# Retention and two MoE layers on one core: the retention's 64x64 matmuls in four quarters of the array, two fixed banks, and two weight tiles fetched earlier

## The chip, the core and the metric

The kernel runs on one core of one Trainium2 chip. The metric is the device time of one execution in microseconds (us). The core's engines are TensorE (PE, with its weight loads shown apart as PEld), VectorE (DVE), ScalarE (ACT), GpSimd (POOL) and SyncE (SP); here SP issues all transfers.

## The reference

What is computed, cut to the core (float32 throughout):

```
scores = q @ k.T / sqrt(64)                      # batch 8, heads 8, sequence 576, head size 64
gamma  = 1 - 2 ** (-5 - head)
ret    = (scores * where(i >= j, gamma ** (i - j), 0)) @ v       # retention, causal with decay
x   = ret, heads side by side                                    # (4608, 512)
h   = max(x @ w1, x @ w2, x @ w3)                                # 512 -> 768
x   = h @ w_out                                                  # 768 -> 512
h   = x @ w_in                                                   # 512 -> 2048
out = (h * clip(h + 3, 0, 6) / 6) @ w_out2                       # 2048 -> 512
```

The weights arrive as float64 words, and the kernel turns them into pairs of float32 parts on the chip.

## The kernel before

**Retention.** A unit is one batch and one pair of heads (e = 0, 1): 8 batches x 4 pairs = 32 units. The sequence is cut into nine chunks of C = 64 positions. For each chunk and head there are three kinds of 64x64 products: *scores* (keys times queries, L217), *outer* products (keys times values, the chunk's contribution to the running state, L225), and *values* (L260: masked scores and old state, stacked to 128 rows, times values and queries). Between them DVE multiplies the scores by a mask (`masked`, L238), adds up the states one chunk after the other (`states`, L251 and L253), and scales the result (`decayed`, L264).

The two heads of a unit lie in the two halves of a tile `raw` (128 partitions). A 64x64 matmul uses one quarter of the 128x128 array: the half of the rows is that of the partitions its operands lie in, the half of the columns is that of the PSUM partitions it writes. Writing (row, column) for a quarter's first row and column, scores of e = 0 and 1 lie in (64, 0) and (0, 64), and outer products of e = 1 and 0 lie in (64, 0) and (0, 64) as well. `keys(n)` issues, chunk by chunk for four chunks, two scores and two outer products, all into bank `at`n, four chunks of scores in its left half and four of outer products in its right half. A matmul of `values` takes all 128 rows and one half of the columns.

The first four units (class `Summed`) run by themselves at the start. Each of the other 28 is done in three steps, `first` (keys(0)), `second` (keys(1), values of chunks 0 to 3, scores of chunk 8) and `third` (values of chunks 4 to 8); the third step of a unit is issued right behind the first step of the next. Between steps stand blocks of twelve 128x512 matmuls of the first MoE layer (`up`, `down`, L393 to L395). In stage t (a tile of 512 tokens) the MoE blocks of tile t are interleaved with the retention of batch t+1: stage 0 with batch 1, stage 1 with batch 2, stages 2 to 6 with batches 3 to 7. What each engine does stands in program order; nothing is reordered by a planner.

**What a step waits for.** PSUM tiles are banks of 512 columns. Waits are set per bank: DVE may read a bank only behind the last matmul issued into it, and the reverse. In before, keys(1) goes into `at1`, and values and scores of chunk 8 into a new tile in `at0`. A unit's `raw` tile (two buffers) is loaded by SP behind the third step of the unit before the last, and ACT scales its keys (`decay`, L188) before the outer products may start.

**Weights.** A class `Weights` fetches float64 tiles (`ws`, three buffers, L93) and turns them into float32 pairs in a pipeline of DVE, ACT and POOL. `wa` does the first layer's 24 tiles during stage 0. `wb_part` does the second layer's 32 tiles; its steps are called by `background()` at every fourth block of stages 1 to 6. Its first step comes at the start of stage 1 and fetches its own first two tiles; on SP they stand behind the four stores `x2d<-y` of tile 0, and DVE's L110 waits for them.

Of the kernel before, what the change touches and what calls it, by code (L numbers as in the profile page):

```python
# [7 lines left out]
F32 = mybir.dt.float32  # L8
# [22 lines left out]
VS1, Z0, KT, KN = 0, S, 2 * S, 3 * S  # L31
# [5 lines left out]
def retention_moe_moe2(ctx: ExitStack, tc, hi, lo, w_a, w_b, mask, qdec, kdec, grow, out):  # L37
    nc = tc.nc
# [33 lines left out]
    def acc_tiles():  # L72
        return [ps_acc.tile([P, 512], F32, tag=f"o{m}", name=f"o{m}") for m in range(4)]
# [3 lines left out]
    mask_sb = at.tile([P, HP, C], F32, name="mask_sb")  # L77
# [60 lines left out]
    def pair():  # L138
        return moe.tile([P, 2, 512], F32R, tag="hy", bufs=8, name="y")
# [7 lines left out]
    wb_part = Weights(w_b, order_b, lambda i: pair())  # L147
# [4 lines left out]
    halves = (slice(0, D), slice(D, P))  # L152
# [32 lines left out]
    def decay(i):  # L185
        if i < len(units):
            k = raws[i][:, KN:HI]
            nc.scalar.mul(k, k, kdec_sb[:, units[i][1], 0:1])  # L188

    xs, xe, ys = {}, {}, {}  # L190

    class Unit:

        def __init__(self, i, banks=None):
            self.i = i
            self.b, self.hp = units[i]
            self.banks = banks

        def begin(self):
            self.ps = self.banks or [ps_at.tile([P, 512], F32, tag=f"at{n}", name=f"at{n}") for n in range(2)]

        def again(self, n):
            if not self.banks:
                self.ps[n] = ps_at.tile([P, 512], F32, tag=f"at{n}", name=f"at{n}")

        def part(self, e, c, first, second):

# [3 lines left out]
        def scores(self, c, ps, c0):  # L213
            t = raws[self.i]
            for e in range(2):
                own, other = halves[e], halves[1 - e]
                nc.tensor.matmul(ps[own, c0:c0 + C], lhsT=t[other, KT + c * C:KT + (c + 1) * C],  # L217
                                 rhs=self.part(e, c, Z0, Z1)[other, :], start=True, stop=True)

        def outer(self, c, ps, c0):  # L220
# [5 lines left out]
                                 rhs=self.part(e, c, VS0, VS1)[own, :], start=True, stop=True)  # L226

        def keys(self, n):
            for c in range(4):
                self.scores(4 * n + c, self.ps[n], c * C)  # L230
                self.outer(4 * n + c, self.ps[n], (4 + c) * C)

        def masked(self, c, n, ps, p0):
            t = raws[self.i]
            for e in range(2):
                own = halves[e]
                c0 = (Z0, Z1)[e] + c * C
                nc.vector.tensor_tensor(  # L238
                    out=t[own, c0:c0 + n * C].rearrange("p (c s) -> p c s", s=C),
                    in0=ps[own, p0:p0 + n * C].rearrange("p (c s) -> p c s", s=C),  # L240
                    in1=mask_sb[own, self.hp, None, :].to_broadcast([D, n, C]), op=ALU.mult)

        def states(self, n):
            for c in range(4 * n, 4 * n + 4):
                for e in range(2):
                    other = halves[1 - e]
                    new, old = (self.part(e, c + d, VS0, VS1)[other, :] for d in (1, 0))
                    c0 = (4 + c - 4 * n) * C
                    add = self.ps[n][other, c0:c0 + C]
                    if c == 0:  # L250
                        nc.vector.tensor_copy(new, add)  # L251
                    else:
                        nc.vector.scalar_tensor_tensor(  # L253
                            out=new, in0=old, scalar=gamma[2 * self.hp + e] ** C, in1=add, op0=ALU.mult, op1=ALU.add)
# [13 lines left out]


        def first_mm(self):  # L270
            self.begin()
            self.keys(0)

        def first_rest(self):
# [2 lines left out]

        def second_mm(self):
            self.keys(1)
            self.again(0)  # L280
            self.values(range(4), self.ps[0])
            self.scores(NC - 1, self.ps[0], 4 * C)

        def second_rest(self):
            self.masked(4, 4, self.ps[1], 0)
            self.states(1)
            self.masked(NC - 1, 1, self.ps[0], 4 * C)
            self.y = at.tile([P, S], F32, tag="yr", bufs=2, name="yr")
            self.decayed(0, 4, self.ps[0])

        def third_mm(self):
            self.again(1)
            self.values(range(4, NC), self.ps[1])

        def third_rest(self):
            self.decayed(4, NC - 4, self.ps[1])
            self.finish()

        def finish(self):
# [8 lines left out]
    class Summed(Unit):  # L308

        def __init__(self, i, banks):
            super().__init__(i, banks)

        def prepare(self):
            for c in range(NC - 1):
                k = raws[self.i][:, KN + c * C:KN + (c + 1) * C]
                nc.scalar.mul(k, k, kdec_sb[:, self.hp, c:c + 1])

        def keys_mm(self):  # L320
            self.begin()
            t = raws[self.i]
            for c in range(NC - 1):
                self.scores(c, self.ps[0], c * C)
            for c in range(NC - 1):
                for e in (1, 0):
                    own, other = halves[e], halves[1 - e]
                    n = NC - 1 - c
                    nc.tensor.matmul(
                        self.ps[1][other, c * C:].rearrange("p (n d) -> p n d", d=D),  # L330
                        lhsT=t[own, KN + c * C:KN + (c + 1) * C],
                        rhs=self.part(e, c, VS0, VS1)[own, None, :].to_broadcast([C, n, D]),
                        start=(c == 0), stop=(c == NC - 2))
# [10 lines left out]
                    in1=grow_sb[other, self.hp, :, None].to_broadcast([D, NC - 1, D]), op=ALU.mult)  # L344

        def values_mm(self):
            self.scores(NC - 1, self.ps[1], 0)
            self.values(range(NC - 1), self.ps[0])

        def values_rest(self):  # L350
            self.masked(NC - 1, 1, self.ps[1], 0)
            self.y = at.tile([P, S], F32, tag="yr", bufs=2, name="yr")
            self.decayed(0, NC - 1, self.ps[0])

        def last_mm(self):
            self.values([NC - 1], self.ps[1], C)

        def last_rest(self):
            self.decayed(NC - 1, 1, self.ps[1], C)
            self.finish()  # L360

    def steps(b):

        us = [Unit(b * HP + hp) for hp in range(HP)]
        res = []
        for hp in range(HP + 1):
            u, last = (us[hp] if hp < HP else None), (us[hp - 1] if hp else None)

            def begin(u=u, last=last):
                if u:  # L370
                    u.first_mm()
                if last:
                    last.third_mm()
                if u:
                    u.first_rest()
                if last:
                    last.third_rest()
                load_raw(b * HP + hp_of(u, last) + 1)

            res.append(begin)  # L380
            if u:
                res.append(lambda u=u: (u.second_mm(), u.second_rest(), decay(u.i + 1) if u.hp < HP - 1 else None))
        return res

    def hp_of(u, last):
        return u.hp if u else HP
# [59 lines left out]
    with tc.manual_schedule():  # L446
# [11 lines left out]
        nc.scalar.mul(rebias, rebias, 2.0 ** 23)  # L458
        xs[0] = x_tile()
        spare = acc_tiles()  # L460
        pairs = [[ps_at.tile([P, 512], F32, tag=f"at{n}", name=f"at{n}") for n in range(2)], spare[:2], spare[2:],
                 [ps_mm.tile([P, 512], F32, tag="mm", name="mm") for n in range(2)]]
        us = [Summed(i, pairs[i]) for i in range(HP)]
        wa.step()
# [23 lines left out]
        def prepare(t):  # L488

            if t >= B:  # L490
                return []
            xs[t] = x_tile()
            decay(t * HP)
            return steps(t)


        side = prepare(1)
        ahead = [lambda f=f, j=j: up(1, f, j) for f in range(3) for j in range(3)]
        for n, blk in enumerate(blocks(0) + [lambda: down(0, F1 - 1)]):
            while wa.steps < min(n + 3, NA + 2):  # L500
                wa.step()
            blk()
            if wa.steps < NA + 2:
                wa.step()
            if side:
                side.pop(0)()
            elif n >= 11 and ahead and n * 9 // 13 > (n - 1) * 9 // 13:
                ahead.pop(0)()
        while ahead:
            ahead.pop(0)()  # L510
# [17 lines left out]
        for t in range(1, TT):  # L528
            side = prepare(t + 1)
# [95 lines left out]
        for t in range(TT):  # L625
            for f in range(F2):
                if f == 4:
                    load_x2(t + 1)
                ps = hidden(t, f)
# [68 lines left out]
```

## Time and profile before

| | |
|---|---|
| median of 3 runs | 1586.28 us (1585.41 to 1587.09) |
| the profiled execution's own time | 1587.3 us |
| its span, first to last instruction | 1585.2 us |
| mean granted TensorE clock | 0.989 |
| busy: PE, PEld, DVE, ACT, POOL | 97%, 79%, 49%, 21%, 10% of the span |

Busy shares are means over stages that differ: at the start transfers and DVE set the pace, later TensorE. A busy PE is not an engine at its peak, since matmuls are pipelined and several can be in flight. Each float32 matmul leaves two records on PE (and two weight loads on PEld), so "x4" in a row of L217 is two matmuls; the MoE's matmuls leave one.

### The profile page before, as it was taken

How to read it: one execution, taken by the hardware profiler on the slowest of the kernel's cores; microseconds unless marked ns; L12 is line 12 of the kernel's file. 1: busy time of each engine (PE TensorE's matmuls, PEld its weight loads, DVE VectorE, ACT ScalarE, POOL GpSimd, SP SyncE). 2: the span in 40 equal slices, each digit the busy share in tenths (PEclk: the TensorE clock that was granted, in tenths of full speed). 3: DMA queues.
4: the chain of work that ended last, by engine and by line, in shares of the span. 5: the costliest groups of instructions: out<-in, count | busy, mean ns of one | idle time of the engine just before them, and what ended most of it. 6: DMA issues, size and time to landing. Idle time of an engine off the chain costs nothing.

```text
span 1585.2 us, 22461 instructions
## 1 busy us (share of the span) xinstructions
PE 1541.1 (97%) x9376; PEld 1257.9 (79%) x9376; DVE 775.4 (49%) x1641; ACT 330.2 (21%) x601; POOL 155.0 (10%) x180
## 2 busy tenths in 40 slices
PE   7789899999999999999999999999999999999998
PEld 5567778888888888888888888888888888888886
DVE  4887476757666666312243334333433333333432
ACT  3344223232323232111111111111111111111111
POOL 1445112222222121000000000000000000000000
PEclk9899999999999999999999999999999999999999
DMA  9573256564655554426430202020010202020001
GB/s 218 140 171 103 80 140 199 138 199 126 193 144 176 142 174 113 146 101 236 161 134 0 80 0 80 1 80 1 30 50 1 80 0 80 0 80 1 27 0 27
DMA packets 48581, 152.73 MB, mean 96 GB/s; under 512 B 13216, under 2 KB 13728, under 8 KB 43232
## 3 DMA queue, kind: packets, MB, share of 16 engines
q1 hardware_dynamic: 48480, 151.31, 31.7%
q8 instruction: 73, 1.20, 0.3%
q14 instruction: 28, 0.23, 0.0%
HBM read 104.10 MB, written 47.19 MB: 95 GB/s over the span
## 4 chain that ended last, share of the span: by engine, by line
PE 91%; DVE 4%; DMA 3%; ACT 1%; issue 0%; SPq 0%; POOL 0%; DVEq 0%; POOLq 0%; ACTq 0%
PE mm L393 18%; PE mm L394 17%; PE mm L395 17%; PE o L591 8%; PE o L593 8%; PE o L592 8%; PE o L393 3%; PE o L394 3%; PE o L395 3%; PE at L217 2%; PE at L260 2%; PE at L225 1%; DMA raw<-in_lo 1%; DMA room<-in_lo 1%; DVE raw L253 1%; DMA ws<-in_w_a 1%
## 5 line engine op out<-in xcount | busy, mean ns | idle before, releaser
L393 PE MATMUL mm<-x,w 128*128 128x512 f32 x1224 | 486.6, 398 | 3.9 <-ACT t L408 3.5
L394 PE MATMUL mm<-x,w 128*128 128x512 f32 x1224 | 479.6, 392 | 0.0
L395 PE MATMUL mm<-x,w 128*128 128x512 f32 x1224 | 479.5, 392 | 0.0
L393 PEld LDWEIGHTS mm<-x,w 128*128 128x128 f32 x1224 | 230.8, 189 | 56.8 <-ACT t L408 4.4
L395 PEld LDWEIGHTS mm<-x,w 128*128 128x128 f32 x1224 | 230.9, 189 | 50.4
L394 PEld LDWEIGHTS mm<-x,w 128*128 128x128 f32 x1224 | 231.1, 189 | 47.6
L579 DVE TENSOR_SCALAR g<-mm 128x512 f32<-128x512 f32 x144 | 99.6, 692 | 342.8 <-PE mm L395 342.6
L52 ACT CAST gh<-g 128x512 fp32r<-128x512 f32 x144 | 89.4, 621 | 683.3 <-DVE g L580 683.3
L591 PE MATMUL o<-w,gh 128*128 128x512 f32 x576 | 225.0, 391 | 0.0
L593 PE MATMUL o<-w,gl 128*128 128x512 f32 x576 | 224.9, 390 | 0.0
L592 PE MATMUL o<-w,gh 128*128 128x512 f32 x576 | 224.7, 390 | 0.0
L53 DVE TENSOR_TENSOR gl<-g,gh 128x512 fp32r<-128x512 f32 x144 | 99.7, 693 | 113.0 <-ACT gh L52 109.0
L410 DVE TENSOR_TENSOR t<-mm,t 128x512 f32<-128x512 f32 x108 | 74.5, 689 | 159.1 <-PE mm L395 158.8
L593 PEld LDWEIGHTS o<-w,gl 128*128 128x128 f32 x576 | 108.1, 188 | 23.4
L592 PEld LDWEIGHTS o<-w,gh 128*128 128x128 f32 x576 | 108.2, 188 | 23.3
L591 PEld LDWEIGHTS o<-w,gh 128*128 128x128 f32 x576 | 108.2, 188 | 23.2
L125 POOL TENSOR_TENSOR wf<-wf,wp 128x512 f32<-128x512 f32 x56 | 74.5, 1331 | 376.4 <-DVE wp L123 358.2
L580 DVE SCALAR_TENSOR_TENSOR g<-g,mm 128x512 f32<-128x512 f32 x144 | 99.1, 688 | 4.9
L238 DVE TENSOR_TENSOR raw<-at,mask_sb 64x64 f32<-64x64 f32 (+2 forms) x172 | 61.3, 356 | 65.4 <-PE at L225 56.4
L253 DVE SCALAR_TENSOR_TENSOR raw<-raw,at 64x64 f32<-64x64 f32 x392 | 85.6, 218 | 11.0
L393 PE MATMUL o<-h,w 128*128 128x512 f32 x216 | 86.2, 399 | 0.0
L217 PE MATMUL at<-raw 64*64 64x64 f32 x1044 | 71.4, 230 | 14.3 <-DMA raw<-in_hi 6.1
(76 smaller groups left out, 1215.1 us busy)
## 6 DMA issues: line engine op xcount, KB each, us to landing
x2d<-y SPq DMA_DIRECT2D x36, 512.0 KB, 3.9
x<-x2d SPq DMA_DIRECT2D x9, 2048.0 KB, 7.9
ws<-in_w_b SPq DMA_DIRECT2D x32, 512.0 KB, 7.5
wbd<-y SPq DMA_DIRECT2D x32, 512.0 KB, 3.2
w<-wbd SPq DMA_DIRECT2D x32, 512.0 KB, 6.1
raw<-in_hi SPq DMA_DIRECT2D x29, 560.0 KB, 5.5
raw<-in_lo SPq DMA_DIRECT2D x29, 560.0 KB, 7.7
ws<-in_w_a SPq DMA_DIRECT2D x24, 512.0 KB, 3.8
```

Source lines behind the costliest of these rows:

```text
L52: nc.scalar.copy(hi, full)
L53: late.append(lambda: (eng or nc.vector).tensor_tensor(out=lo, in0=full, in1=f32(hi), op=ALU.subtract))
L217: nc.tensor.matmul(ps[own, c0:c0 + C], lhsT=t[other, KT + c * C:KT + (c + 1) * C], rhs=self.part(e, c, Z0, Z1)[other, :], start=True, stop ...
L253: nc.vector.scalar_tensor_tensor(out=new, in0=old, scalar=gamma[2 * self.hp + e] ** C, in1=add, op0=ALU.mult, op1=ALU.add)
L393: nc.tensor.matmul(ps, lhsT=wh, rhs=xh, start=first, stop=False)
L394: nc.tensor.matmul(ps, lhsT=wh, rhs=xl, start=False, stop=False)
L395: nc.tensor.matmul(ps, lhsT=wl, rhs=xh, start=False, stop=last)
L579: nc.vector.tensor_scalar(out=g, in0=ps, scalar1=3.0, scalar2=0.0, op0=ALU.add, op1=ALU.max)
L580: nc.vector.scalar_tensor_tensor(out=g, in0=g, scalar=6.0, in1=ps, op0=ALU.min, op1=ALU.mult)
L591: nc.tensor.matmul(acc[s], lhsT=gh[:, c], rhs=w[:, 0, :], start=(f == 0), stop=False)
L592: nc.tensor.matmul(acc[s], lhsT=gh[:, c], rhs=w[:, 1, :], start=False, stop=False)
L593: nc.tensor.matmul(acc[s], lhsT=gl[:, c], rhs=w[:, 0, :], start=False, stop=(f == F2 - 1))
```

## The change

Scores move to the quarters (64, 64) and (0, 0), so that a chunk's four 64x64 products lie in four different quarters. All scores go into one fixed bank (`at0`, columns by chunk) and all outer products into the other (`at1`); both are allocated once instead of anew for each step. The mask's two halves are exchanged, since scores of e now come out in the other half of the partitions. In the second step the scores of chunk 8 are issued ahead of the values, and these go into `at1`. The values of chunks 4 to 7 go into `at0` and that of chunk 8 into `at1`, so that `decayed` takes two instructions there (256 and 64 columns) instead of one (320). The first two tiles of `w_b` are fetched at block 21 of stage 0.

```diff
-    xs, xe, ys = {}, {}, {}
+    xs, xe = {}, {}
+    banks = [ps_at.tile([P, 512], F32, name=f"at{n}") for n in range(2)]
...
             for e in range(2):
-                own, other = halves[e], halves[1 - e]
-                nc.tensor.matmul(ps[own, c0:c0 + C], lhsT=t[other, KT + c * C:KT + (c + 1) * C],
+                other = halves[1 - e]
+                nc.tensor.matmul(ps[other, c0:c0 + C], lhsT=t[other, KT + c * C:KT + (c + 1) * C],
                                  rhs=self.part(e, c, Z0, Z1)[other, :], start=True, stop=True)
...
         def keys(self, n):
-            for c in range(4):
-                self.scores(4 * n + c, self.ps[n], c * C)
-                self.outer(4 * n + c, self.ps[n], (4 + c) * C)
+            for c in range(4 * n, 4 * n + 4):
+                self.scores(c, self.ps[0], c * C)
+                self.outer(c, self.ps[1], c * C)
...
         def second_mm(self):
             self.keys(1)
-            self.again(0)
-            self.values(range(4), self.ps[0])
-            self.scores(NC - 1, self.ps[0], 4 * C)
+            self.scores(NC - 1, self.ps[0], 0)
+            self.values(range(4), self.ps[1])
...
         def third_mm(self):
-            self.again(1)
-            self.values(range(4, NC), self.ps[1])
+            self.values(range(4, NC - 1), self.ps[0], 4 * C)
+            self.values([NC - 1], self.ps[1], 4 * C)
 
         def third_rest(self):
-            self.decayed(4, NC - 4, self.ps[1])
+            self.decayed(4, 4, self.ps[0], 4 * C)
+            self.decayed(NC - 1, 1, self.ps[1], 4 * C)
             self.finish()
...
         def values_mm(self):
-            self.scores(NC - 1, self.ps[1], 0)
-            self.values(range(NC - 1), self.ps[0])
+            self.scores(NC - 1, self.ps[0], 0)
+            self.values(range(NC - 1), self.ps[1])
...
             if side:
                 side.pop(0)()
-            elif n >= 11 and ahead and n * 9 // 13 > (n - 1) * 9 // 13:
+            if n == 21:
+                wb_part.fetch(2)
+            if not side and n >= 11 and ahead and n * 9 // 13 > (n - 1) * 9 // 13:
                 ahead.pop(0)()
...
-    mask = mask.transpose(1, 2, 0, 3).reshape(P, HP, C).astype(np.float32)
+    mask = mask[:, ::-1].transpose(1, 2, 0, 3).reshape(P, HP, C).astype(np.float32)
```

On PE, this is the end of the second step of batch 3's first unit in the program before (out<-in by names, size, count of matmuls; the numbers behind `at` are those of the tiles):

```order
L217 MATMUL at_3180<-raw 64x64 x2
L225 MATMUL at_3180<-raw 64x64 x2
L260 MATMUL at_3266<-raw 64x64 x8
L217 MATMUL at_3266<-raw 64x64 x2
L393 MATMUL mm<-x,w 128x512
```

And this is the same end of a second step in the program of the change, where scores are L212, outer products L220, values L254 and the MoE's first matmul L382:

```order
L212 MATMUL at_128<-raw 64x64 x2
L220 MATMUL at_129<-raw 64x64 x2
L212 MATMUL at_128<-raw 64x64 x2
L254 MATMUL at_129<-raw 64x64 x8
L382 MATMUL mm<-x,w 128x512
```

The scores of chunk 8 have moved from behind the values to ahead of them, next to the other 64x64 matmuls; scores and outer products now name two different tiles.

On SP, the end of stage 0 and the start of stage 1 before:

```order
L93 DMA ws<-in_w_a 128x512 x8
L428 DMA x2d_66<-y 256x1x512 x4
L93 DMA ws<-in_w_b 128x512 x2
L165 DMA raw<-in_hi 64x2240
L168 DMA raw<-in_lo 64x2240
```

And the same place of the change (the stores are L417 there):

```order
L93 DMA ws<-in_w_a 128x512 x8
L93 DMA ws<-in_w_b 128x512 x2
L417 DMA x2d_66<-y 256x1x512 x4
L165 DMA raw<-in_hi 64x2240
L168 DMA raw<-in_lo 64x2240
```

The two fetches of `w_b` have passed the four stores; everything else on SP keeps its place.

## Rows read from the trace of the kernel before

**Rows 1.** Windows by stage: stretch, length, busy us by engine (instructions), granted clock, DMA share, GB/s.

```profile
51.00:125.00 74.00, 63.05 (x586) 49.49 (x584) 58.74 (x165) 30.94 (x57) 30.05 (x31) 0.90 0.61 149
...
183.00:240.00 57.00, 51.37 (x554) 40.91 (x553) 37.90 (x121) 11.46 (x22) 5.31 (x11) 0.94 0.55 139
240.00:640.00 400.00, 400.00 (x3454) 325.74 (x3453) 266.69 (x742) 122.12 (x224) 81.56 (x96) 1.00 0.54 159
```

**Rows 2.** Timeline of PE, a second step: start, us, engine, line, tiles, forms, records [idle].

```profile
305.64 0.33 PE L217 MATMUL at<-raw 64*64 64x64 f32 x4
...
305.92 0.28 PE L217 MATMUL at<-raw 64*64 64x64 f32 x4
...
306.50 0.28 PE L225 MATMUL at<-raw 64*64 64x64 f32 x4
306.72 0.69 PE L260 MATMUL at<-raw 128*64 128x64 f32 x16
307.33 0.33 PE L217 MATMUL at<-raw 64*64 64x64 f32 x4
307.59 0.50 PE L393 MATMUL mm<-x,w 128*128 128x512 f32 x1
```

**Rows 3.** Timeline of PE in the first units, where 64x512 outer products begin.

```profile
26.71 0.59 PE L329 MATMUL o<-room 64*64 64x512 f32 x1
26.76 0.22 PE L217 MATMUL o<-room 64*64 64x64 f32 x1
26.82 1.02 PE L329 MATMUL o<-room 64*64 64x512 f32 x3
```

**Rows 4.** Timeline of DVE, end of stage 0 and start of stage 1.

```profile
162.08 0.68 DVE L123 SCALAR_TENSOR_TENSOR wp<-ws,wp 128x512 uint32<-128x512 uint32 x1
...
188.76 0.43 DVE L110 TENSOR_SCALAR wp<-ws 128x512 uint32<-128x512 uint32 x1 [8.48 <-DMA ws<-in_w_b]
```

**Rows 5.** Timeline of SP's issues, same place.

```profile
178.51 3.48 SPq L428 DMA_DIRECT2D x2d<-y  x4
182.04 2.52 SPq L93 DMA_DIRECT2D ws<-in_w_b  x2
...
202.13 0.60 SPq L168 DMA_DIRECT2D raw<-in_lo  x1
```

**Rows 6.** Timeline of PE in stage 1.

```profile
183.87 0.33 PE L217 MATMUL at<-raw 64*64 64x64 f32 x4
...
192.93 1.12 PE L260 MATMUL at<-raw 128*64 128x64 f32 x16 [3.88 <-DVE raw L253]
...
194.38 0.79 PE L393 MATMUL o<-h,w 128*128 128x512 f32 x1
...
199.52 0.33 PE L217 MATMUL at<-raw 64*64 64x64 f32 x4
...
201.33 0.50 PE L393 MATMUL o<-h,w 128*128 128x512 f32 x1
...
204.30 0.33 PE L217 MATMUL at<-raw 64*64 64x64 f32 x4
...
210.45 0.33 PE L225 MATMUL at<-raw 64*64 64x64 f32 x4 [0.51 <-ACT raw L188]
```

**Rows 7.** Windows, one stretch of stage 1, columns as in rows 1.

```profile
193.00:199.00 6.00, 6.00 (x31) 4.80 (x32) 4.19 (x15) 1.24 (x2) 0.00 (x0) 0.50 0.01 3
```

**Rows 8.** Timeline of ACT, the scaling of the third unit's keys.

```profile
209.68 0.72 ACT L188 ACTIVATE raw<-raw,kdec_sb 128x512 f32<-128x512 f32 x1 [5.01 <-DMA raw<-in_lo]
```

**Rows 9.** Timeline of PE in stage 1, the last unit's third step.

```profile
233.59 0.80 PE L260 MATMUL at<-raw 128*64 128x64 f32 x20 [1.15 <-DVE raw L238]
```

**Rows 10.** Groups of DVE's L264 by form: count, busy us, mean ns, idle before.

```profile
L264 DVE TENSOR_TENSOR yr<-at,qdec_sb 128x320 f32<-128x320 f32 x28 | 13.4, 480 | 7.2 <-PE at L260 7.1
L264 DVE TENSOR_TENSOR yr<-at,qdec_sb 128x256 f32<-128x256 f32 x28 | 11.9, 425 | 0.7
...
L264 DVE TENSOR_TENSOR yr<-mm,qdec_sb 128x64 f32<-128x64 f32 x1 | 0.2, 215 | 0.0
```

More of the change, by code (lines that the diff above doesn't have):

```diff
@@ L188, in decay, with __init__ @@
             nc.scalar.mul(k, k, kdec_sb[:, units[i][1], 0:1])
-    xs, xe, ys = {}, {}, {}
+    xs, xe = {}, {}
+    banks = [ps_at.tile([P, 512], F32, name=f"at{n}") for n in range(2)]
     class Unit:
-        def __init__(self, i, banks=None):
+        def __init__(self, i, banks):
             self.i = i
             self.b, self.hp = units[i]
[L199 to L206, printed above, removed]
+            self.ps = banks
         def part(self, e, c, first, second):
@@ L235, in masked @@
             for e in range(2):
-                own = halves[e]
+                own, other = halves[e], halves[1 - e]
                 c0 = (Z0, Z1)[e] + c * C
@@ L239, in masked @@
                     out=t[own, c0:c0 + n * C].rearrange("p (c s) -> p c s", s=C),
-                    in0=ps[own, p0:p0 + n * C].rearrange("p (c s) -> p c s", s=C),
-                    in1=mask_sb[own, self.hp, None, :].to_broadcast([D, n, C]), op=ALU.mult)
+                    in0=ps[other, p0:p0 + n * C].rearrange("p (c s) -> p c s", s=C),
+                    in1=mask_sb[other, self.hp, None, :].to_broadcast([D, n, C]), op=ALU.mult)
         def states(self, n):
@@ L247, in states @@
                     new, old = (self.part(e, c + d, VS0, VS1)[other, :] for d in (1, 0))
-                    c0 = (4 + c - 4 * n) * C
-                    add = self.ps[n][other, c0:c0 + C]
+                    add = self.ps[1][other, c * C:(c + 1) * C]
                     if c == 0:
@@ L270, in first_mm @@
         def first_mm(self):
-            self.begin()
             self.keys(0)
@@ L279, in second_mm @@
             self.keys(1)
-            self.again(0)
-            self.values(range(4), self.ps[0])
-            self.scores(NC - 1, self.ps[0], 4 * C)
+            self.scores(NC - 1, self.ps[0], 0)
+            self.values(range(4), self.ps[1])
         def second_rest(self):
-            self.masked(4, 4, self.ps[1], 0)
+            self.masked(4, 4, self.ps[0], 4 * C)
             self.states(1)
-            self.masked(NC - 1, 1, self.ps[0], 4 * C)
+            self.masked(NC - 1, 1, self.ps[0], 0)
             self.y = at.tile([P, S], F32, tag="yr", bufs=2, name="yr")
-            self.decayed(0, 4, self.ps[0])
+            self.decayed(0, 4, self.ps[1])
         def third_mm(self):
-            self.again(1)
-            self.values(range(4, NC), self.ps[1])
+            self.values(range(4, NC - 1), self.ps[0], 4 * C)
+            self.values([NC - 1], self.ps[1], 4 * C)
         def third_rest(self):
-            self.decayed(4, NC - 4, self.ps[1])
+            self.decayed(4, 4, self.ps[0], 4 * C)
+            self.decayed(NC - 1, 1, self.ps[1], 4 * C)
             self.finish()
@@ L308, in retention_moe_moe2 @@
     class Summed(Unit):
-        def __init__(self, i, banks):
-            super().__init__(i, banks)
         def prepare(self):
@@ L320, in keys_mm @@
         def keys_mm(self):
-            self.begin()
             t = raws[self.i]
@@ L346, in values_mm @@
         def values_mm(self):
-            self.scores(NC - 1, self.ps[1], 0)
-            self.values(range(NC - 1), self.ps[0])
+            self.scores(NC - 1, self.ps[0], 0)
+            self.values(range(NC - 1), self.ps[1])
         def values_rest(self):
-            self.masked(NC - 1, 1, self.ps[1], 0)
+            self.masked(NC - 1, 1, self.ps[0], 0)
             self.y = at.tile([P, S], F32, tag="yr", bufs=2, name="yr")
-            self.decayed(0, NC - 1, self.ps[0])
+            self.decayed(0, NC - 1, self.ps[1])
         def last_mm(self):
-            self.values([NC - 1], self.ps[1], C)
+            self.values([NC - 1], self.ps[0], C)
         def last_rest(self):
-            self.decayed(NC - 1, 1, self.ps[1], C)
+            self.decayed(NC - 1, 1, self.ps[0], C)
             self.finish()
     def steps(b):
-        us = [Unit(b * HP + hp) for hp in range(HP)]
+        us = [Unit(b * HP + hp, banks) for hp in range(HP)]
         res = []
@@ L460, in retention_moe_moe2 @@
         spare = acc_tiles()
-        pairs = [[ps_at.tile([P, 512], F32, tag=f"at{n}", name=f"at{n}") for n in range(2)], spare[:2], spare[2:],
+        pairs = [banks, spare[:2], spare[2:],
                  [ps_mm.tile([P, 512], F32, tag="mm", name="mm") for n in range(2)]]
```

## The prediction, made before the changed kernel was run

> **What bounds the kernel now.** I read the windows by stage first. From 240 to 640 us, where batches 3 to 7 are worked on (20 units), PE is busy in 400.00 of 400.00 us at the full clock, and DVE in 266.69 [rows 1]: whatever PE is spared there shortens the kernel. Behind 640 us there is no retention, and the change touches nothing. Between 51 and 125 us (batch 1, four units) PE is busy in 63.05 of 74.00 us and DVE in 58.74, so neither is full and waits decide. Between 183 and 240 us (batch 2, four units) PE lacks 5.6 of 57.00 us, and its mean clock is 0.94.
>
> Then I read the timeline of that stretch. DVE sits idle for 8.48 us until 188.76 for the first tile of w_b [rows 4]; SP had issued that tile at 182.04, behind four stores that took it from 178.51 [rows 5]. Behind DVE's L110 are queued the mask and the states of batch 2's first unit, and PE's values wait for these for 3.88 us [rows 6]. After the wait PE runs at 0.50 of its clock, the lower level of 1.2 GHz, from 193 to 199 us [rows 7].
>
> Last I read one step of the full stretch, for what the 64x64 matmuls cost. A group of four records (two matmuls) starts at 305.92 and the sixth group from there ends the series at 306.50: five gaps in 0.58 us, 0.116 us each [rows 2].
>
> **Do quarters run side by side?** The records of the first units say yes for two. A 64x512 matmul record starts at 26.71 and lasts 0.59 us, one of 64x64 lasts 0.22: 0.37 us for 448 columns more, so a column occupies a quarter for 0.83 ns and a 64-column record for 53 ns. While that long record runs, an L217 record starts at 26.76 and the other quarter's long record at 26.82 [rows 3]: each quarter works through its own matmuls. It fits with the 0.116 us: two matmuls of two records, 2 x 53 = 106 ns and a little for each start, done in the time of one. Values go side by side too: 16 records in 0.61 us to the next line's start [rows 2], 38 ns each, less than 53, though all of them use all the rows. So two halves of the rows, and two halves of the columns, are each seen at work at once; all four quarters are not, because before the scores and outer products share two quarters and must take turns.
>
> **The change part by part.**
>
> *Four quarters.* A call of keys is eight groups: the first starts at 305.64, the values at 306.72, 1.08 us [rows 2]. If scores and outer products of a chunk overlap wholly, four groups' time is saved, 4 x 0.116 = 0.46 us; if they can't overlap, nothing. Four starts must now fit where two did: some 7 ns for each of the two more in eight periods would take back 0.1 (an estimate: 0.116 less 0.106 is 10 ns for four starts in two quarters, so a start costs 2.5 to 7 ns). I take 0.42 to 0.43 between, nearer to full overlap, because rows 3 show that the other quarter needs no turn-taking.
>
> *Scores of chunk 8 ahead of the values.* Before they cost 307.33 to 307.59, 0.26 us with a change of shape [rows 2]. Next to the other scores they are one more group, 0.116. Saved: 0.14 us a unit. Together 2 x 0.43 + 0.14 = 1.0 us a unit, 20 us for the 20 units of the full stretch. Bounds: 0.14 x 20 = 2.9 and (2 x 0.46 + 0.14) x 20 = 21.5.
>
> *Fixed banks.* The mask of a first step now waits until the third step's values in the same bank are through, as do DVE's reads of the states. By PE's order that is about as late as before: the keys end 0.46 earlier, and the values behind them take 0.61 for 16 records. Where steps are two or three blocks apart this is hidden by the blocks; in stage 1 there is one block between some steps (201.33 to 204.30 [rows 6]), DVE's chain of mask and states fills it, and I allow 0.3 us there.
>
> *One more instruction of DVE.* 320 columns took 480 ns; 256 take 425 and 64 take 215 [rows 10]: 0.16 us a unit, 4.5 us in all. In the full stretch 266.69 of 400 us hides it. In stage 0, where DVE is among the bounds, four units may cost 0.6; PE's saving may give as much back. I take 0.5 lost, with 2 gained as the other end.
>
> *The two w_b tiles.* Three buffers hold weight tiles; DVE last reads the first layer's at 162.08 + 0.68 [rows 4]. From there SP may fetch, so the tiles are issued near 163, not 182.04, and land long before 180.28, where DVE's wait of 8.48 us began. The stores behind them are hardly later, for they wait for data until 178.51 [rows 5]. What is late next? PE's keys begin at 183.87 [rows 6] and end 0.62 us later, so DVE's mask may start at 184.5. From L110 at 188.76 to the values at 192.93 DVE took 4.17 us, 0.43 of them L110's [rows 4, 6]; behind the keys that is 3.74 at most, 188.2. PE would have issued the values at 192.93 - 3.88 = 189.05; two calls of keys less and one group more make it 188.2 as well. So the wait of 3.88 us goes, and with it the low clock: the block of 12 from 194.38 to 199.52 took 5.14 us, the like block at full clock 201.33 to 204.30 took 2.97; values and scores before it took 1.45 (192.93 to 194.38) against 0.87 (306.72 to 307.59) [rows 2, 6]. That is 3.88 + 2.17 + 0.58 = 6.6 us.
>
> *What follows in stage 1.* PE would reach the third step of batch 2's first unit 6.6 us earlier, and by some 1.4 more from three calls of keys and one move: 8. That step frees a raw buffer, and from its end (201.33) to the third unit's outer products (210.45) the chain is a load, issued at 202.13 and landing at 209.68, and ACT's scaling of 0.72 [rows 5, 6, 8]: 9.1 us that the change doesn't shorten. PE, 0.6 us quicker in between, waits that much longer there than its 0.51, but keeps the 8. The next steps add about 1. At the end of the last unit PE waits 1.15 us for DVE's L238 [rows 9]: there DVE sets the pace, PE's savings are lost and DVE's longer work costs 0.2. So stage 1 gives 9, between 7 (no overlap of quarters) and 10.
>
> *The first four units* have the same move of a 64x64 pair, ahead of values that wait for DVE anyway; I count nothing.
>
> **The sum.** 20 + 9 - 0.5 = 28.5 us. The profiled execution took 1587.3 (span 1585.2), 1.0 above the median of the runs. 1587.3 - 28.5 = 1558.8, or by the median 1586.28 - 28.5 = **1557.8 us**. Two in a thousand, 3.2 us, is about what a measurement of this kernel can tell from no change.
>
> **Rivals.**
>
> *Four quarters don't overlap.* Two quarters that share a half of the columns write into the same PSUM partitions; no row of before shows two matmuls ending there at once. Nor is a series shown with starts closer on average than 0.116 / 4 = 29 ns [rows 2], though four quarters would need 15. If either limits, keys gain nothing, and what is left is 2.9 + 7 - 0.5 = 9.4: 1576.9. For it speaks that the mean of 29 ns is the least in the trace; against it, that starts in rows 3 lie 50 ns apart without regard to one another. The Trainium skill (TensorE: Matmul & The Clock Gate, "Wait — 56ns, not 53.3ns?") has such a floor: start-to-start never below about 25 ns however small the matmul. By that, an estimate: 32 records save 4 ns each, 0.13 us a call, 1571 or so. Another page of the Trainium skill (TensorEngine Tiling (Array Packing), "Key Properties") has tiles of the array run loads and matmuls independently; the trace agrees for two quarters.
>
> *Turning between pairs of quarters costs a drain.* This ends slower. From the last group of keys at 306.50 to the values is 0.22 instead of 0.116 [rows 2]: a change of shape costs 0.10. Were a change from one column half to the other under the same rows such a turn, each chunk would have two, 160 chunks in the full stretch, 320 x 0.10 = 32 us, against the 9.4 left: 1586.3 + 22.6 = 1609. It decides from 0.03 us a turn. Against it: before, values switch column halves at every matmul without a pause.
>
> *The quarters overlap, but the early fetch moves the wait.* DVE's chain or the raw load could take back most of stage 1's gain, for instance if the low clock came anyway in the longer wait for L188. Then 9 becomes 3: 1563.8. Against it: the wait of 1.15 us at 233.59 was followed by full clock in rows 1's next stretch.
>
> **How the numbers follow.** Forecast 0.66, no overlap 0.20 (a third of it near 1571), turns 0.07, moved wait 0.07. The predicted time is 1557.8. The lowest sum is 21.5 + 10 + 2 = 33.5, 1552.8. From 1552 up to 1577 the range holds the forecast, the moved wait and nearly all of no overlap; without the last, its own range is 1552 to 1564. All but the turns are faster by more than 3.2 us; of these I move 0.01 to "same", and 0.01 of the turns, for prices near the break-even, to "same" as well: faster 0.92, same 0.02, slower 0.06.
>
> **What would show it.** Four quarters: eight records in 0.116 to 0.13 us, and a second step that takes 1.4 us from its first score to the next MoE matmul instead of 1.95 (305.64 to 307.59); PE still full from 240 us to an end some 20 us nearer. The fetch: no wait of DVE for w_b near 180, no 0.50 clock near 195, and a longer wait of PE for ACT's L188. Wrong if records of scores and outer products still come four in 0.116 us, if PE waits in the full stretch for DVE's masks or states, or if gaps appear between the groups.

## The result, and the profile after

The changed kernel took 1565.69 us (median of 4 runs, 1562.15 to 1568.28), the kernel before 1586.09 beside it: a ratio of 0.9869, 95% interval 0.9849 to 0.989. It is faster, by 20.4 us where 28.5 were forecast. The profiled execution took 1565.97 (span 1564.1, mean clock 0.988). About 8 us have to be found. One execution of this kernel in a later experiment (e8) took 7870.4 us, with matmul records some four times as long; why is open, and it enters no ratio.

The MoE matmuls come in the same order in every kernel of this study. So I compare the start of the same matmul (the k-th record of the form 128x512) in two traces. This table gives that difference to the kernel before, in us, at the matmul that stands at the time in the first line there; minus is earlier. Each row is one execution. The experiments' rows are read further down.

| at, in before | 51.90 | 183.09 | 208.20 | 222.18 | 229.43 | 244.00 | 649.03 | 805.15 |
|---|---|---|---|---|---|---|---|---|
| changed kernel | +3.15 | +0.29 | -7.65 | -8.09 | -8.38 | -5.15 | -26.49 | -21.03 |
| e1, fetch alone | +0.51 | -0.05 | -6.80 | -6.07 | -6.07 | -6.08 | -6.08 | -6.08 |
| e2, without the fetch | +1.73 | -0.03 | -1.76 | -0.40 | -0.68 | +3.75 | -17.58 | -12.18 |
| e3, scores back | -0.67 | -4.20 | -10.91 | -10.69 | -10.50 | -8.14 | -11.07 | -5.88 |
| e4, scores of chunk 8 behind | +1.36 | -0.12 | -6.98 | -7.56 | -7.00 | -6.74 | -24.87 | -19.47 |
| e5, gl elsewhere | +3.21 | +0.90 | -7.06 | -5.81 | -6.10 | -3.06 | -24.40 | -24.40 |
| e6, weight step later | -0.19 | -2.42 | -10.35 | -10.89 | -11.18 | -11.87 | -32.43 | -32.43 |
| e7, before with gl late | +0.45 | -3.19 | -3.76 | -3.56 | -3.56 | -3.58 | -3.58 | +3.04 |
| e9, e6's kernel again | +0.29 | -1.75 | -9.72 | -10.05 | -10.33 | -11.05 | -31.63 | -31.63 |

The changed kernel's line reads: stage 0 gives nothing, stage 1 at first 8.7 us and then loses 3.2 of them, stages 2 to 6 give 21.3, and 5.5 are lost at about 800 us, where there is no retention any more. Behind that nothing changes.

The windows by stage of the changed kernel, columns as in [rows 1]:

```profile
51.00:125.00 74.00, 60.17 (x598) 46.32 (x595) 64.41 (x173) 31.12 (x57) 32.60 (x32) 0.89 0.60 156
...
183.00:240.00 57.00, 52.43 (x578) 41.06 (x577) 42.63 (x130) 13.47 (x26) 7.63 (x13) 0.97 0.56 140
240.00:620.00 380.00, 380.00 (x3475) 306.75 (x3474) 272.85 (x761) 120.80 (x222) 79.49 (x95) 1.00 0.57 165
```

PE is still full from 240 us on. One second step there, PE's timeline (scores L212, outer products L220, values L254):

```profile
280.09 0.27 PE L212 MATMUL at<-raw 64*64 64x64 f32 x2
280.10 0.27 PE L220 MATMUL at<-raw 64*64 64x64 f32 x2
...
280.25 0.22 PE L212 MATMUL at<-raw 64*64 64x64 f32 x2
280.26 0.23 PE L220 MATMUL at<-raw 64*64 64x64 f32 x2
280.31 0.23 PE L212 MATMUL at<-raw 64*64 64x64 f32 x2
280.32 0.23 PE L220 MATMUL at<-raw 64*64 64x64 f32 x2
...
280.54 0.23 PE L212 MATMUL at<-raw 64*64 64x64 f32 x2
280.56 0.22 PE L220 MATMUL at<-raw 64*64 64x64 f32 x2
280.60 0.28 PE L212 MATMUL at<-raw 64*64 64x64 f32 x4
280.81 0.69 PE L254 MATMUL at<-raw 128*64 128x64 f32 x16
281.43 0.50 PE L382 MATMUL mm<-x,w 128*128 128x512 f32 x1
```

Scores and outer products now start as pairs 10 to 20 ns apart, and four records come every 58 ns (280.25 to 280.54 in five periods) where four took 116 ns [rows 2]. The step takes 281.43 - 280.09 = 1.34 us, before 1.95.

In stage 1 the fetch did its work. DVE's and then SP's timeline there, to be set beside [rows 4, 5]:

```profile
180.49 0.42 DVE L110 TENSOR_SCALAR wp<-ws 128x512 uint32<-128x512 uint32 x1
180.82 0.42 DVE L111 TENSOR_SCALAR wf<-ws 128x512 uint32<-128x512 uint32 x1
```

```profile
153.96 5.15 SPq L93 DMA_DIRECT2D ws<-in_w_b  x2
178.81 3.47 SPq L417 DMA_DIRECT2D x2d<-y  x4
194.21 0.54 SPq L165 DMA_DIRECT2D raw<-in_hi  x1
```

L110 waits for nothing, and the stores are issued 0.3 us later than before, as all of this trace is there (+0.29). What is late next stands at the end of the stage. DVE's timeline around the last unit of batch 2:

```profile
216.45 0.86 DVE L233 TENSOR_TENSOR raw<-at,mask_sb 64x256 f32<-64x256 f32 x2 [0.89 <-PE at L254]
...
219.69 0.41 DVE L110 TENSOR_SCALAR wp<-ws 128x512 uint32<-128x512 uint32 x1
220.02 0.41 DVE L111 TENSOR_SCALAR wf<-ws 128x512 uint32<-128x512 uint32 x1
220.36 0.68 DVE L121 SCALAR_TENSOR_TENSOR wf<-ws,wf 128x512 f32<-128x512 uint32 x1
220.96 0.68 DVE L123 SCALAR_TENSOR_TENSOR wp<-ws,wp 128x512 uint32<-128x512 uint32 x1
...
222.16 1.32 DVE L53 TENSOR_TENSOR xe<-yr,xe 128x64 fp32r<-128x64 f32 x1
...
224.38 1.95 DVE L247 SCALAR_TENSOR_TENSOR raw<-raw,at 64x64 f32<-64x64 f32 x8
226.35 0.46 DVE L233 TENSOR_TENSOR raw<-at,mask_sb 64x64 f32<-64x64 f32 x2
```

And PE's, which waits for that last mask:

```profile
223.71 0.39 PE L384 MATMUL mm<-x,w 128*128 128x512 f32 x1
226.86 0.80 PE L254 MATMUL at<-raw 128*64 128x64 f32 x20 [2.77 <-DVE raw L233]
227.60 0.50 PE L382 MATMUL mm<-x,w 128*128 128x512 f32 x1
...
229.42 0.63 PE L384 MATMUL mm<-x,w 128*128 128x512 f32 x1
...
231.56 0.41 PE L383 MATMUL mm<-x,w 128*128 128x512 f32 x1
```

DVE has hardly a gap from 216.45 to 226.8, and 1.9 us of it (219.69 to 221.56, the next instruction) are a step of `w_b`, L110 to L123, queued ahead of the unit's second mask and states. The step costs DVE more than that. POOL's product in the same step is this row:

```profile
221.78 1.62 POOL L125 TENSOR_TENSOR wf<-wf,wp 128x512 f32<-128x512 f32 x1 [4.79 <-DMA raw<-in_hi]
```

The small subtraction `xe` of DVE, which starts beside it, takes 1.32 us and ends 0.08 us behind it. The ten traces of the table and of before have 320 such subtractions: 270 start beside no product of POOL and take 0.21 to 0.22 us; of the 50 that start beside one, 49 take 1.27 to 1.32 us and end 0.08 to 0.09 us behind it. So the product holds them up, here for 1.1 us; by what is not tested. The kernel before has the same step and the same 1.32 us at this place (229.47 there), so neither is new; but before, PE came to it later.

PE waits 2.77 us, before 1.15 [rows 9], and then runs at the lower level of 1.2 GHz (mean clock 0.65 from 227 to 231): from 227.60 to 231.56 ten matmuls take 3.96 us, which at the 0.23 us between starts of a full clock are 2.3 to 2.4. 2.77 - 1.15 + 1.6 = 3.2, the loss in the table.

The second loss is at the start of the second MoE (`gated`, `project`), first PE, then DVE:

```profile
770.11 0.39 PE L583 MATMUL o<-w,gh 128*128 128x512 f32 x1
774.14 0.66 PE L584 MATMUL o<-w,gl 128*128 128x512 f32 x1 [3.64 <-DVE gl L53]
774.60 0.63 PE L582 MATMUL o<-w,gh 128*128 128x512 f32 x1
...
777.89 0.39 PE L584 MATMUL o<-w,gl 128*128 128x512 f32 x1
```

```profile
766.24 0.69 DVE L571 SCALAR_TENSOR_TENSOR g<-g,mm 128x512 f32<-128x512 f32 x1
773.39 0.69 DVE L53 TENSOR_TENSOR gl<-g,gh 128x512 fp32r<-128x512 f32 x1 [6.47 <-DMA x2d<-y]
```

The first `gl` tile may be written only when the last store `x2d<-y` of the first MoE has landed, because it lies in the room of that `y` tile. In the kernel before, the second `gl` tile lay there. DVE waited for the same store, but PE was busy through that wait and did not stop; the row of DVE in that trace:

```profile
800.13 0.69 DVE L53 TENSOR_TENSOR gl<-g,gh 128x512 fp32r<-128x512 f32 x1 [4.03 <-DMA x2d<-y]
```

The rooms are given out when the program is built. In the changed program two rooms of the ring of eight that the h and y tiles share are exchanged, first at the 26th of 122 tiles and so also at the last one, that `y`. The wait of 3.64 us is followed by the lower clock again (mean 0.57 from 774 to 778).

### The profile page after: what moved, and what is told of

Its sections match the earlier page's. It is cut to its first block, busy times and chain, and to the rows that moved or that the text cites. A ratio compares the mean times of both kernels' runs of the same rounds, so it can differ in the third digit from the quotient of the medians.

```text
span 1564.1 us, 22512 instructions
## 1 busy us (share of the span) xinstructions
PE 1515.7 (97%) x9376; PEld 1229.8 (79%) x9376; DVE 787.7 (50%) x1669; ACT 330.3 (21%) x601; POOL 155.2 (10%) x180
## 4 chain that ended last, share of the span: by engine, by line
PE 89%; DVE 5%; DMA 3%; issue 1%; POOL 1%; ACT 0%; SPq 0%; POOLq 0%; DVEq 0%; ACTq 0%
PE mm L382 18%; PE mm L384 17%; PE mm L383 17%; PE o L584 8%; PE o L582 8%; PE o L583 8%; PE o L382 3%; PE o L383 3%; PE o L384 3%; PE at L254 2%; PE at L212 2%; DMA raw<-in_lo 1%; DMA room<-in_lo 1%; DVE raw L247 1%; DVE raw L233 1%
## 5 line engine op out<-in xcount | busy, mean ns | idle before, releaser
L382 PE MATMUL mm<-x,w 128*128 128x512 f32 x1224 | 487.3, 398 | 3.5 <-ACT t L397 3.1
L382 PEld LDWEIGHTS mm<-x,w 128*128 128x128 f32 x1224 | 231.4, 189 | 56.4 <-ACT t L397 3.9
L584 PEld LDWEIGHTS o<-w,gl 128*128 128x128 f32 x576 | 108.5, 188 | 27.5 <-DVE gl L53 4.1
L382 PE MATMUL o<-h,w 128*128 128x512 f32 x216 | 85.2, 394 | 0.0
L383 PE MATMUL o<-h,w 128*128 128x512 f32 x216 | 84.1, 390 | 0.0
```

The costliest lines, as they stand in the source:

```text
L382: nc.tensor.matmul(ps, lhsT=wh, rhs=xh, start=first, stop=False)
L383: nc.tensor.matmul(ps, lhsT=wh, rhs=xl, start=False, stop=False)
L584: nc.tensor.matmul(acc[s], lhsT=gl[:, c], rhs=w[:, 0, :], start=False, stop=(f == F2 - 1))
```

## Experiments

My theory after the result: the retention's steps gain all that was forecast or more, through the overlap of four quarters; what is missing is a w_b step ahead of the last unit's mask in stage 1, and a room of a tile at the start of the second MoE. The rivals: the fixed banks are the gain and not the quarters; the last unit's own chain on DVE is too long; the fetch causes the late start of the second MoE.

**e1, the kernel before with the early fetch alone.**

```diff
-            elif n >= 11 and ahead and n * 9 // 13 > (n - 1) * 9 // 13:
+            if n == 21:
+                wb_part.fetch(2)
+            if not side and n >= 11 and ahead and n * 9 // 13 > (n - 1) * 9 // 13:
```

> The kernel before with the early fetch of two w_b tiles alone. If the fetch takes away the wait of 3.88 us and the low clock behind it for good: 6.6 us less, about 1579.5 us. If most of that comes back at the third step of the batch's last unit, where TensorE waits for VectorE (2.8 us in the changed kernel's trace, 1.15 us before): 3 us less, about 1583. If the fetch is also what swaps two rooms of the ring of h and y tiles, the first gl tile of MoE2 waits for a store and 5.5 us come on top: about 1585 to 1588.

Measured 1580.89 us, ratio 0.9962 (0.995 to 0.9974): 5.7 us by the medians (before 1586.56 beside it) and 6.0 in stage 1 by the table. Of the 6.6 worked out for the wait and its low clock, 0.7 go again between 208 and 222 us (-6.80, -6.07): at the third unit PE waits 0.81 us for its load `raw<-in_lo` (203.54 in that trace), ahead of the 0.51 for L188, which stay. The wait at the last unit's third step is 1.14 us, as before. Nothing is lost at 800 us, so the fetch does not exchange the rooms.

**e2, the changed kernel without the fetch.**

```diff
-            if n == 21:
-                wb_part.fetch(2)
```

> The changed kernel without the early fetch. If the 20 units of stages 2 to 6 give 21.3 us by themselves and the banks' part also swaps the two rooms, so that MoE2 begins 5.5 us late, with the wait for w_b and its low clock back: stage 1 about 1.5 us shorter, in sum 17.3 us less, about 1569 us. If it is the fetch that swaps the rooms: no loss at MoE2, about 1563. If the quarters need the fetch, no theory here: above 1575.

Measured 1574.84 us, ratio 0.9924 (0.9912 to 0.9937): 6 us more than expected. Stages 2 to 6 give 21.33 and the start of the second MoE loses 5.40, as thought. The error is in stage 1, which is not 1.5 us shorter but 3.8 longer. Its timeline of PE:

```profile
186.64 0.39 PE L382 MATMUL mm<-x,w 128*128 128x512 f32 x1
...
190.81 0.48 PE L212 MATMUL at<-raw 64*64 64x64 f32 x4 [3.33 <-DVE raw L233]
192.81 0.37 PE L220 MATMUL at<-raw 64*64 64x64 f32 x2 [1.53 <-DVE raw L247]
...
234.56 1.33 PE L254 MATMUL at<-raw 128*64 128x64 f32 x20 [2.79 <-DVE raw L233]
```

Most of it is the last row: at the last unit's third step 4.4 us go (-0.68 at 229.43, +3.75 at 244.00), as 3.2 do in the changed kernel, and I had left that out. The first two rows show what the fixed banks do. With them the second keys write into the banks that DVE still reads for the first step's mask and states. When DVE is held by the w_b tile (8.27 us here), PE stops already ahead of the keys, twice, for 4.86 us, where before it stopped ahead of the values, for 3.88 [rows 6]. No loss of time is to be seen from it: at 208 us e2 is 1.76 us ahead of before, a little more than the 1.5 expected. Behind that 1.4 us go up to 222 us, where the changed kernel gains 0.4. There PE waits 0.45, 0.42 and 0.51 us at the third unit's keys (207.96 to 209.54 in that trace) and then runs at a mean clock of 0.62 from 209.5 to 214; the changed kernel waits 0.43 and 0.51 there and keeps the full clock.

So the fetch is worth more with the rest of the change than by itself: by the table 3.75 + 5.15 = 8.9 us in place of 6.0 (by the medians, each against its own before, 20.4 - 11.7 = 8.7). The difference lies in two places of e2's trace: 1.8 us behind the third unit, of which 0.42 are a wait that the changed kernel has not and most of the rest the lower clock, and 1.2 us at the last unit, where the waits are alike (2.79 and 2.77) and the lower clock lasted longer.

**e3, the scores back in the quarters of the outer products, all else as in the changed kernel.**

```diff
-                other = halves[1 - e]
-                nc.tensor.matmul(ps[other, c0:c0 + C], lhsT=t[other, KT + c * C:KT + (c + 1) * C],
+                own, other = halves[e], halves[1 - e]
+                nc.tensor.matmul(ps[own, c0:c0 + C], lhsT=t[other, KT + c * C:KT + (c + 1) * C],
...
-                    in0=ps[other, p0:p0 + n * C].rearrange("p (c s) -> p c s", s=C),
-                    in1=mask_sb[other, self.hp, None, :].to_broadcast([D, n, C]), op=ALU.mult)
+                    in0=ps[own, p0:p0 + n * C].rearrange("p (c s) -> p c s", s=C),
+                    in1=mask_sb[own, self.hp, None, :].to_broadcast([D, n, C]), op=ALU.mult)
...
-    mask = mask[:, ::-1].transpose(1, 2, 0, 3).reshape(P, HP, C).astype(np.float32)
+    mask = mask.transpose(1, 2, 0, 3).reshape(P, HP, C).astype(np.float32)
```

> The changed kernel with the scores back in the two quarters that the state products use (output on its own half again, mask halves not exchanged); banks, the moved scores of chunk 8 and the fetch stay. If the four quarters overlap and that is the gain of a keys call (0.43 us, 40 calls): 17.3 us come back, about 1583 us. If the gain comes from the fixed banks (score and state product of a chunk in different banks), nothing comes back: about 1566. In between: shared.

Measured 1584.12 us, ratio 0.9983 (0.9972 to 0.9994). In stages 2 to 6 it gains 2.93 us in place of 21.34. PE's timeline of a second step:

```profile
297.06 0.33 PE L212 MATMUL at<-raw 64*64 64x64 f32 x4
297.23 0.28 PE L220 MATMUL at<-raw 64*64 64x64 f32 x4
297.34 0.28 PE L212 MATMUL at<-raw 64*64 64x64 f32 x4
...
298.04 0.28 PE L212 MATMUL at<-raw 64*64 64x64 f32 x4
298.26 0.69 PE L254 MATMUL at<-raw 128*64 128x64 f32 x16
```

Four records take 0.116 us again, though scores and outer products lie in two banks. So the banks alone give nothing; with two banks, the quarters give (21.34 - 2.93) / 40 = 0.46 us a call of keys. Four quarters with one bank were not run, so whether the two banks are needed for it stays open. The 2.93 that stay are the moved scores of chunk 8, 0.15 us a unit.

**e4, the scores of chunk 8 behind the values again.**

```diff
-            self.scores(NC - 1, self.ps[0], 0)
             self.values(range(4), self.ps[1])
+            self.scores(NC - 1, self.ps[0], 0)
```

> The changed kernel with the scores of chunk 8 behind the values of the second step again, as before the change. If their place ahead of the values is worth 0.14 us in each of 20 units: 2.8 us more, about 1568.5 us. If it is worth nothing: 1565.7. The second step became 0.61 us shorter in the trace where a first step became 0.46 shorter, which speaks for 0.15.

Measured 1570.24 us, ratio 0.9896 (0.9883 to 0.9909), 1.7 us more than expected. Stages 2 to 6 give 18.13 us, 3.2 less: 0.16 us a unit. With e3's 2.93 from the other side, the two parts make up the 21.3.

This trace shows something else by chance. At the last unit's third step of stage 1 it loses only 0.3 us (-7.00, -6.74), though the step of `w_b` stands ahead of the mask here too. DVE's row and PE's:

```profile
223.29 0.21 DVE L53 TENSOR_TENSOR xe<-yr,xe 128x64 fp32r<-128x64 f32 x1
```

```profile
226.86 0.80 PE L254 MATMUL at<-raw 128*64 128x64 f32 x20 [1.40 <-DVE raw L233]
```

It is the one `xe` of the fifty that POOL's product did not hold up. PE's wait is 1.40 us in place of 2.77, 1.1 of the difference being `xe`, and the clock stays at 1.00 from 226 to 232. So without the hold the four instructions of the weights cost little, as far as one execution shows it. It took 1567.55 us; the other three took 1569.84 to 1571.80 and have no trace.

**e5, the changed kernel with an unused tile ahead of the gl tiles.**

```diff
-        m2 = None
+        m2, pads = None, []
...
+            if not pads:
+                pads.append(m2.tile([P, 3 * TB], F32, tag="pad", name="pad"))
             gl = m2.tile([P, TB], F32R, tag="gl", bufs=3, name="gl")
```

> The changed kernel with an unused tile of 6 KB per partition ahead of the gl tiles in MoE2's pool, so that the first gl tile no longer lies in the room of the last stored y tile. If that room is what makes MoE2 begin late: the 3.6 us wait at the first product with gl and the half clock behind it go, 5.4 us less than the changed kernel, about 1560.3 us. If the store would have been late for somebody anyway (the second gh tile still lies in that room): 1565.7.

Measured 1558.02 us, ratio 0.9838 (0.9817 to 0.9859). The loss at 800 us is gone whole (-24.40 ahead of it and behind); stage 1 of this execution gave 4.0 us where the changed kernel's gave 5.4, with the same program there. The difference is the clock: behind waits of 0.45 and 0.51 us at the third unit (202.66 and 204.06) it was 0.51 from 205 to 208.5, and between 208 and 222 us of the table 1.25 go where the changed kernel, behind waits of 0.43 and 0.51, gains 0.44. The store is still late for somebody, ACT's second `gh`, but ahead of that PE has products to do. ACT's timeline:

```profile
769.05 0.62 ACT L52 CAST gh<-g 128x512 fp32r<-128x512 f32 x1 [2.08 <-DVE g L571]
775.17 0.62 ACT L52 CAST gh<-g 128x512 fp32r<-128x512 f32 x1 [5.50 <-DMA x2d<-y]
```

**e6, the changed kernel with one w_b step behind the last unit's third step.**

```diff
-                if t < 7 and n % 4 == 0:
+                if t < 7 and (n in (0, 4, 10, 12) if t == 1 else n % 4 == 0):
```

> The changed kernel with the third w_b step of stage 1 put behind the third step of the batch's last unit (two blocks later), and the fourth where it was. If those instructions of VectorE (some 2 us) are what makes TensorE wait 2.8 us at the last unit's third step: the wait falls under 1 us, the half clock behind it does not come, and stage 1 ends 8 us shorter than before in place of 5.2. If the unit's own chain of mask, states and outputs is too long by itself: 5.2 stays. This order of allocations also gives the last stored y tile the room that it had before the change, so MoE2's 5.4 us should go with it: 1557 us by the first, 1560.3 by the second.

Measured 1555.98 us, ratio 0.9829 (0.9808 to 0.985). Stage 1 gives 11.87 - 2.42 = 9.45 us in place of 5.4, and the second MoE starts without loss, since this order of tiles gives the last `y` its old room. The window of stage 1 and, below it, PE's last third step there:

```profile
183.00:240.00 57.00, 54.88 (x595) 43.24 (x594) 44.43 (x133) 15.56 (x29) 8.88 (x14) 1.00 0.54 133
```

```profile
221.72 0.80 PE L254 MATMUL at<-raw 128*64 128x64 f32 x20 [0.45 <-DVE raw L233]
```

The wait is 0.45 us, and the mean clock of the stage is 1.00. So it was the step of the weights, its four instructions together with the `xe` that its product on POOL holds up; here both stand behind the unit's masks (`xe` takes 1.31 us at 225.42, and PE does not wait for it). The unit's own chain is short enough.

**e7, the kernel before with the first gl tile in the room of the last stored y tile.**

```diff
-        m2 = None
+        m2, pads = None, []
...
+            if not pads:
+                pads.append(m2.tile([P, TB], F32, tag="pad", name="pad"))
             gl = m2.tile([P, TB], F32R, tag="gl", bufs=3, name="gl")
```

> The kernel before with an unused tile of 2 KB per partition ahead of the gl tiles, which puts the first gl tile of MoE2 into the room of the last stored y tile and changes nothing else. If a room alone costs the 5.4 us: about 1592 us, with a wait of 3.6 us at the first product with gl. If something else in the changed kernel makes the store late or the wait dear: 1586.5.

Measured 1591.15 us, ratio 1.004 (1.0026 to 1.0054): slower by the room of one tile, which touches no computation. PE's timeline shows the changed kernel's wait:

```profile
793.02 0.39 PE L594 MATMUL o<-w,gh 128*128 128x512 f32 x1
797.21 0.80 PE L595 MATMUL o<-w,gl 128*128 128x512 f32 x1 [3.80 <-DVE gl L53]
797.80 0.63 PE L593 MATMUL o<-w,gh 128*128 128x512 f32 x1
```

The table gives 3.04 + 3.58 = 6.6 us there, of which 3.8 are the wait and the rest the lower clock behind it.

**e8 and e9, the changed kernel and e6's kernel on one chip.**

> The changed kernel itself, beside the next one on one chip. Its start (up to 183 us) has differed by some 5 us between executions, the rest by a few tenths: 1562 to 1568 us, about 20.5 us less than before.

> The kernel with the third w_b step of stage 1 two blocks later, beside the changed kernel on one chip. By the traces stage 1 ends 4.3 us earlier than the changed kernel's and MoE2 begins without the 5.4 us: 9.5 us less than the changed kernel, about 30 us less than before. If the two differ by under 4 us, the traces showed no more than differences between starts.

Measured 1566.24 us, ratio 0.9878 (0.9857 to 0.9899), and 1557.35 us, ratio 0.9826 (0.9808 to 0.9844). The kernel with the later weight step is 8.9 us faster than the changed one and 27.5 faster than before, 2.5 less than expected. Its trace (stage 1: 9.30, stages 2 to 6: 20.58, second MoE: no loss) repeats e6's.

## Why the prediction came out as it did

The direction and the main mechanism were right; the sum was 8 us too good. The measured 1565.69 lies in the range of 1552 to 1577, but above the 1552 to 1564 that the prediction calls its own range without the rival of no overlap. The wider range was there for that rival, which did not come true. The result lies in it because of two losses that the sum did not have, so that the range held is luck.

- **Four quarters overlap: right, and a little undersized.** Four records in 58 ns and 0.46 us a call of keys (e3), the upper bound; I took 0.43, with some 0.03 us for starts (the 7 ns at the upper end of that estimate do not follow from its 10 ns for four starts). No such cost shows. With 0.15 to 0.16 us for the scores of chunk 8 (e3, e4; forecast 0.14), a unit gains 1.07 us, the full stretch 21.3 instead of 20. The rival without overlap and the one with a drain at each turn are refuted by the pairs of rows 10 to 20 ns apart. The Trainium skill (TensorE: Matmul & The Clock Gate, "Wait — 56ns, not 53.3ns?") puts a floor of about 25 ns under the time from start to start; here it does not hold across quarters, where the mean is 58 / 4 = 14.5 ns, and the measurement decides. The Trainium skill (TensorEngine Tiling (Array Packing), "Key Properties") lets different tiles run matmuls in parallel; the rows agree, for all four quarters.
- **The two tiles: right.** The fetch alone gives 6.0 us of the 6.6 (e1). SP issued it at 153.96, 9 us earlier than I had put it, which changes nothing.
- **The raw load behind it: the length right, its sign not.** PE's outer products of the third unit start at 203.33, and the matmul behind the third step of the first, at 201.33 in [rows 6], comes 7.35 us earlier, at 193.98: 9.35 us, before 9.1. But the longer wait for L188 that was named as a sign did not come; it is 0.51 us as before. In its place PE had waited 0.23 and 0.43 us in between, at 197.22 and 202.06, for DVE's reads of the fixed banks.
- **The end of stage 1: the step that failed first.** "PE's savings are lost and DVE's longer work costs 0.2": I read the 1.15 us of [rows 9] as a place where DVE paces and took the loss for small. But PE came 8.7 us earlier to a DVE that had to do the same weight step, with the `xe` held up behind it, and an instruction more in less time; the wait grew to 2.77 us, and the low clock came behind it. Stage 1 gave 5.4 us, not 9. It is the third rival's mechanism (there it was worked out as 3), at another place than L188. e6 shows the cause and gives 9.45; e4 shows that the hold of 1.1 us decided much of it.
- **"Behind 640 us there is no retention, and the change touches nothing": the step that failed second,** for 5.5 us. No instruction there differs; the rooms of the tiles do (e5, e7). It comes with the retention's part of the change (the loss is there in e2, e3 and e4, not in e1), and without the quarters (e3) and without the moved scores (e4) as well; which of the other edits moves the rooms was not separated.
- **The fixed banks** were called hidden, by the third step's values, with 0.3 us allowed in stage 1. The wait that shows is another one: the next keys behind DVE's reads of the same bank. In stage 1 of the changed kernel there are four such waits (0.16, 0.23, 0.43 and 0.23 us at 192.64, 197.22, 202.06 and 219.69), 1.05 us together; before has none, and the full stretch has none.
- **Stage 0 and the first four units: nothing to see.** The +3.15 us at the first MoE matmul are scatter: e2, e4, e5, e6 and e9 have the same start and stand at 1.73, 1.36, 3.21, -0.19 and 0.29, and at 183 us these six lie between +0.90 and -2.42. Up to there whole executions differ by 5 us. In e3, 4.2 us ahead, it goes with the clock: its mean from 51 to 84 us was 0.97, in the changed kernel 0.86. The 0.5 us for DVE's additional instruction can't be told from that.

Together, as the table has them: 5.44 us won in stage 1 and 21.34 in stages 2 to 6, less 0.29 in stage 0 and 5.46 at the second MoE, make 21.0 between the two traces; the medians give 20.4. With the two losses mended, e6 measures 27.7 (1583.72 beside it) and e9 27.5, near the forecast's 28.5.

## What to carry to other kernels

Small matmuls in different quarters of the array ran side by side here even where two write the same PSUM partitions, each pair in a bank of its own, so spread them over all four; but a shared bank that is kept for the next step ties TensorE to the engine that reads it, so look at who is late there. When a stall goes, follow the engine that had been waiting to the next place where it meets the others, and look at what unrelated work is queued ahead there. And compare the rooms that tiles get before and after a change: a later pool may begin on a room that is still being stored.

## What was not expected of the hardware

Starts of 64x64 float32 records in four quarters came 14.5 ns apart on average, with no cost for a turn from one pair to the other. Short waits cost more than themselves, and their length alone does not tell how much. Behind 2.77 us TensorE ran at the lower level and lost 1.6 us more, behind 2.79 in e2 2.8 more, behind 3.64 us 1.7 more (774.14 to 778.11 for ten matmuls). Behind 1.40 us (e4), 1.15 us (before) and 0.45 us (e6) it kept the full clock; behind two waits of 0.45 and 0.51 us in e5 it did not, and that cost 1.7 us against the changed kernel, which had 0.43 and 0.51 there. And a product on POOL held up a small subtraction on DVE beside it in 49 of 50 cases, 1.3 us in place of 0.2; in the fiftieth (e4), PE's wait behind it was 1.40 us where the changed kernel's was 2.77.
